# Last tile's logits ahead of the late tiles' conversions, and gathered blocks and late tiles interleaved, in a three-stage attention, MoE and softplus kernel

## The chip, the cores and the metric

One core of one Trainium2 chip. The metric is the device time of one launch in microseconds. All times inside a trace are counted from the start of the profiled span. The engines are PE (matrix products), ACT, DVE and POOL (elementwise work), and SP, which only issues transfers; POOL and ACT issue some too. Each engine takes its instructions in the order in which they were written and stops at one whose input isn't there.

## What is computed

Three layers follow each other on 2304 tokens (4 batches of 576) with 512 features:

```python
# 1 attention, 8 heads, windowed or dilated mask
scores = np.where(masks[None], scale * q @ k.transpose(0, 1, 3, 2), -1e9)
x = softmax(scores) @ v                    # -> (2304, 512)
# 2 mixture of 8 experts, one expert for each token
e_idx = np.argmax(x @ w_gate, axis=1)
for e in range(8):
    h = np.maximum(x[mask_e] @ w1[e], 0.0)
    out[mask_e] = gate_w[mask_e, None] * eom[mask_e, e, None] * (h @ w2[e])
# 3 dense layer with softplus between two products
g = np.maximum(h, 0.0) + np.log1p(np.exp(-np.abs(h)))      # h = out @ w_in
y = g @ w_out
```

## The kernel before

**Attention by tiles.** The tokens are cut into 20 tiles (tile 14 and tile 19, the fifth of their batches, have 64 rows, the others of interest here 128). A loop runs over steps i = 0 to 21. Step i starts tile i, finishes the attention of tile i-1, and for tile i-2 transposes x on PE (`transpose_x`, L485, into `px`) and copies it on ACT (`evict_x`, L496, into `xT`). Steps 20 and 21 are the tail, in which no new tile starts.

**Routing by groups.** The tiles form six groups; the last, group 5, is tiles 17 to 19. For each group `logits` and `route` take the logits on PE (`pl`, L506, from `xT`), transpose them (`lt` L522 and L525 on DVE, `plt` L528 on PE), pick each token's expert on DVE (L565 to L616), count places with five small matmuls (`prk`, L592 to L596), and end with each token's place and its factor in `pair` (L616). They are written as a generator whose steps are interleaved with other work; `("go", 5, n)` in the table of events takes n steps of it, `pump()` takes a few.

**The first expert's rows.** The expert that is computed first (rank 0) is picked before all tiles are routed. Its tokens, up to 424, are brought into `xacc`, four blocks of 128 features by 424 places (c = 0 to 3), transposed and scaled, in two ways that add up in the same accumulators:

- Tokens of tiles 0 to 13 are gathered from memory by POOL's indirect transfers into `xg` 0 to 3 (three of 128 rows, one of 40), and `mm_gathered` multiplies each with a diagonal matrix (L962), one matmul of the order's listing for each c and block.
- Tokens of the late tiles 14 to 19 are loaded by SP (`load_late`, L982, tile `xl0`), scaled and split in two on ACT and DVE (`split_late`: `h` L993, `l` L995), and multiplied with a 0/1 selection matrix (`sel_late`, `sel`, L1004; `mm_late`, L1014). That is two matmuls of 424 columns for each c and late tile. Tiles 14 and 19 share one pair of buffers, one half each.

`xl0` has five buffers for six late tiles; the load of tile 19 waits for the buffer of tile 15, which is free after `l` of tile 15. When `xacc` is complete, `split_rank0` copies it to `xh` on ACT (L1027) and takes the rest as `xl` on DVE (L732), four pieces each. The first expert's first product (`ph`, L894) starts after the last of them. `wl` (L732 as well) is the low part of the first expert's weights; when one is done SP may load the next weight piece.

**Order.** It is written out by hand: engines run what the Python code emits, in that order. Events are put at places of the loop with `at(step, place, ...)`: `ll` is `load_late`, `se` `sel_late`, `sp` `split_late`, `mg` `mm_gathered`, `az` a first matmul that zeroes `xacc` 0 or 1, `q` a `wl`. After the loop a list `late` emits the rest of the late work.

Of the kernel before, what the change touches and what calls it, by code (L numbers as in the profile page):

```python
# [21 lines left out]
P = 128  # L22
# [15 lines left out]
CAPS = [424, 392, 344, 328, 312, 288, 280, 256]  # L38
# [4 lines left out]
def attn_moe_softplus_kernel(ctx: ExitStack, tc: tile.TileContext, q, k, v, w_gate, w_ogate, w1, w2, w_in, w_out, out, dbg=None):  # L43
    nc = tc.nc
# [9 lines left out]
    NC = DM // P  # L54
# [3 lines left out]
    GROUPS = [(0, 4), (4, 8), (8, 11), (11, 14), (14, 17), (17, 20)]  # L58
# [274 lines left out]
    bg, PUMP = [], [2, 1]  # L333

    def pump(times=None):
        for e in bg[: PUMP[1]]:
            if e[1] > 0:
                e[1] -= 1
                continue
            for _ in range(PUMP[0] if times is None else times):  # L340
                e[1] = next(e[0], None)
                if e[1] is None:
                    bg.remove(e)
                if e[1] != 0:
                    break
# [476 lines left out]
    def piece_lo(r, j, eng=None):  # L822
        d = pieces[r, j]
        sub(eng or nc.vector, d[2], d[0], d[1])
# [4 lines left out]
    xg, xs = {}, {}  # L829

    def ntile(n):
        return (n + P - 1) // P
# [103 lines left out]
    NL = GROUPS[G_DRAM][1]  # L936
    xacc = {}
# [8 lines left out]
    def acc(c):  # L946
        pool, tag = ((ps_s, "s"), (ps_s, "s"), (ps_o, "o"), (ps_t, "tp"))[c]
        xacc[c] = pool.tile([P, 512], F32, tag=tag, name=f"xacc{c}")

    def acc0(c):  # L950
        acc(c)
        zero = bce(cumb[:, 0], CAPS[0] // NE)
        nc.tensor.matmul(xacc[c][:, : CAPS[0]], ones, zero, start=True, stop=False, skip_group_check=True)

    def mm_gathered(cs):
        for c in cs:
            if c not in xacc:
                acc0(c)
        for t in range(ntile(CAPS[0])):
            rows = min(P, CAPS[0] - P * t)  # L960
            for c in cs:
                nc.tensor.matmul(  # L962
                    xacc[c][:, P * t : P * t + rows],
                    xg[0, t][:rows, P * c : P * c + P],
                    xacc["d", t][:rows, :rows],
                    start=False,
                    stop=False,
                    skip_group_check=True,
                )

    def rows_of(i):
        return P if i % NW < NW - 1 else S % P
# [33 lines left out]
    def mm_late(i, cs, which=(0, 1)):  # L1006
        last = i == len(tiles) - 1
        parts, s_ = xacc["l", i], xacc["s", i]
        for c in cs:
            first_ = c not in xacc  # L1010
            if first_:
                acc(c)
            for k_ in which:
                nc.tensor.matmul(  # L1014
                    xacc[c][:, : CAPS[0]],
                    parts[k_][:, P * c : P * c + P],
                    s_,
                    start=first_ and k_ == 0,
                    stop=(last and k_ == 1),
                    skip_group_check=True,  # L1020
                )
# [17 lines left out]
    def load_next():  # L1039

        nload[1] += 1
        while nload[1] and nload[0] < len(order_):
            r, j = order_[nload[0]]
            two = r == NE and j >= DIRECT
            if two and nload[1] < 2:
                break
            if r not in er and r != NE:
                if not K.get("ranked"):
                    break
                er[r] = tab_load(nc.sync, r, NE - 1)  # L1050
            load_piece(r, j, er.get(r))
            nload[0] += 1
            nload[1] -= 1 + two

    def hi_(r, j):
        piece_hi(r, j)

    def lo_(r, j):
        piece_lo(r, j)
        if r != NE or j >= 4:  # L1060
            load_next()
# [18 lines left out]
    n = len(tiles)  # L1080
# [12 lines left out]
    def at(i, s, *evs):  # L1093
        EV.setdefault((i, s), []).extend(evs)

    at(21, 0, ("az", 0), ("az", 1))
    at(21, 1, ("mg", 0))
    for g, (t0, t1) in enumerate(GROUPS):
        if g >= G_FAST:
            for t in range(t0, t1):  # L1100
# [5 lines left out]
    at(18, 4, ("ll", 15))  # L1106
    at(19, 3, ("ll", 16), ("ll", 17))
    at(20, 2, ("sc", 0), ("sc", 1), ("sc", 2), ("sc", 3))
    at(20, 3, ("se", 14), ("se", 15), ("sp", 15, "hl"), ("sp", 14, "h"), ("se", 16), ("sp", 16, "h"), ("ll", 18), ("ll", 19))
    at(21, 1, ("go", 5, 4), ("sp", 16, "l"), ("mg", 1), ("go", 5, 8), ("sp", 14, "l"))  # L1110
    ordering = order()

    def events(i, s):
        for what, *a in EV.get((i, s), ()):
            if what == "r":
                bg.append([group(*a), 0, *a])
            elif what == "pl":
                logits_of(*a)
            elif what == "h":
                hi_(0, *a)  # L1120
            elif what == "q":
                lo_(0, *a)
            elif what == "sc":
                diag_gathered(*a)
            elif what == "az":
                acc0(*a)
            elif what == "mg":
                mm_gathered(a)
            elif what == "ll":
                load_late(*a)  # L1130
            elif what == "go":

                e = next((e for e in bg if e[2] == a[0]), None)
                for _ in range(a[1]):
                    if e in bg:
                        e[1] = next(e[0], None)
                        if e[1] is None:
                            bg.remove(e)
            elif what == "se":
                g = next(g for g, (t0, t1) in enumerate(GROUPS) if t0 <= a[0] < t1)  # L1140
                while any(e[2] == g for e in bg):
                    pump()
                sel_late(*a)
            elif what == "sp":
                split_late(*a)

    for i in range(n + 2):
# [52 lines left out]
        if i == n - 4:  # L1200
            nc.vector.tensor_scalar(K["slots"], K["slots"], e0nt, None, ALU.add)
            K["rt"] = K["rt2"]
    def w_lo(i, j):
        lo_(0, j)

    late = []
    for c in (2, 3):
        late += [(mm_late, 15, (c,), (0,)), (mm_gathered, NL, (c,))]
    late += [(mm_late, 15, (c,), (1,)) for c in (2, 3)] + [(mm_late, 15, (c,)) for c in (0, 1)] + [(mm_late, 16, (c,)) for c in range(NC)]
    late += [(fn, i) for fn in (sel_late, split_late) for i in range(17, n)] + [(w_lo, 17, j) for j in (0, 1)]  # L1210
    late += [(mm_late, 17, (c,)) for c in range(NC)]

    late += [(mm_late, i, (c,)) for i, c in ((n - 2, 0), (n - 2, 1), (n - 1, 0), (n - 1, 1), (n - 2, 2), (n - 1, 2), (n - 2, 3), (n - 1, 3))]
    while late:
        if bg:
            pump()
        fn, i, *a = late[0]
        g = next(g for g, (t0, t1) in enumerate(GROUPS) if t0 <= i < t1)
        if fn is mm_gathered or all(e[2] != g for e in bg):
            late.pop(0)  # L1220
            fn(*a) if fn is mm_gathered else fn(i, *a)
    for fn in deferred:
        fn()
    actx.close()
# [91 lines left out]
    for r in range(NE):  # L1316
        n = CAPS[r]
# [73 lines left out]
    sp = {}  # L1391
# [132 lines left out]
```

## Time and profile before

| what | value |
|---|---|
| median of 3 runs | 814.38 us (814.18 to 817.77) |
| profiled run, its time | 815.12 us |
| its span | 813.5 us (1.62 us lie around it) |
| PE busy | 769.4 us, 95% of the span |
| DVE busy | 566.0 us, 70% |
| ACT busy | 471.8 us, 58% |
| POOL busy | 141.3 us, 17% |
| chain that ended last | PE 61%, DVE 11%, issue 9%, ACT 4%, DMA 2% |

Busy shares are averages over all stages. The page's 40 slices are 20.3 us each; the granted PE clock is full in nearly all of them and 0.8 and 0.7 of full in the seventh and eighth, between 122 and 163 us. The change lies in that stretch.

### The profile page before, as it was taken

How to read it: one execution, taken by the hardware profiler on the slowest of the kernel's cores; microseconds unless marked ns; L12 is line 12 of the kernel's file. 1: busy time of each engine (PE TensorE's matmuls, PEld its weight loads, DVE VectorE, ACT ScalarE, POOL GpSimd, SP SyncE). 2: the span in 40 equal slices, each digit the busy share in tenths (PEclk: the TensorE clock that was granted, in tenths of full speed). 3: DMA queues.
4: the chain of work that ended last, by engine and by line, in shares of the span. 5: the costliest groups of instructions: out<-in, count | busy, mean ns of one | idle time of the engine just before them, and what ended most of it. 6: DMA issues, size and time to landing. Idle time of an engine off the chain costs nothing.

```text
span 813.5 us, 14993 instructions
## 1 busy us (share of the span) xinstructions
PE 769.4 (95%) x5542; PEld 689.8 (85%) x5543; DVE 566.0 (70%) x1112; ACT 471.8 (58%) x909; POOL 141.3 (17%) x170
## 2 busy tenths in 40 slices
PE   6998885999999999999989999999999999999994
PEld 5666664898999999999978888899999999999993
DVE  6867884653577887656798989867656656666662
ACT  4776542344655665566766676656656655655561
POOL 9814433121102001100012121210000001001001
PEclk8999998799999999999999999999999999999998
DMA  9996666255799998769431322310000001001000
GB/s 227 267 249 172 137 163 154 72 194 168 241 285 294 306 306 281 234 195 345 109 103 62 96 67 71 91 65 1 20 7 33 0 1 39 1 1 39 1 1 39
DMA packets 85887, 104.49 MB, mean 128 GB/s; under 512 B 30428, under 2 KB 61404, under 8 KB 85792
## 3 DMA queue, kind: packets, MB, share of 16 engines
q1 hardware_dynamic: 74496, 84.22, 35.9%
q0 software_dynamic: 5104, 13.40, 5.1%
q10 hardware_dynamic: 6192, 5.56, 2.0%
q8 instruction: 65, 1.06, 0.6%
q14 instruction: 30, 0.25, 0.1%
HBM read 83.98 MB, written 19.32 MB: 127 GB/s over the span
## 4 chain that ended last, share of the span: by engine, by line
PE 61%; DVE 11%; issue 9%; ACT 4%; DMA 2%; POOL 1%; ACTq 0%; POOLq 0%; DVEq 0%; SPq 0%
PE q L1433 5%; PE pg L895 5%; PE pg L896 5%; PE pg L894 5%; PE q L1431 5%; PE q L1432 5%; PE ph L890 3%; PE ph L892 3%; PE ph L891 3%; PE py L890 3%; PE py L891 3%; PE py L892 3%; DVE l L1411 2%; DVE l L1409 1%; PE py L894 1%
## 5 line engine op out<-in xcount | busy, mean ns | idle before, releaser
L895 PE MATMUL pg<-xlm,wh 128*128 128x384 f32 x384 | 129.7, 338 | 0.0
L894 PE MATMUL pg<-xhm,wh 128*128 128x384 f32 x384 | 129.4, 337 | 0.1
L896 PE MATMUL pg<-xhm,wl 128*128 128x384 f32 x384 | 129.3, 337 | 0.0
L1433 PE MATMUL q<-wh,gl 128*128 128x512 f32 x288 | 114.3, 397 | 3.8 <-DVE gl L732 3.8
L1431 PE MATMUL q<-wh,gh 128*128 128x512 f32 x288 | 114.2, 397 | 1.4 <-ACT gh L1417 0.9
L1432 PE MATMUL q<-wl,gh 128*128 128x512 f32 x288 | 113.2, 393 | 0.0
L732 DVE TENSOR_TENSOR wl<-wr,wh 128x1024 fp32r<-128x1024 f32 x72 | 87.6, 1218 | 32.9 <-ACT wh L787 32.9
L1417 ACT CAST gh<-l 128x384 fp32r<-128x384 f32 x96 | 49.2, 512 | 100.9 <-DVE l L1411 100.9
L732 DVE TENSOR_TENSOR gl<-l,gh 128x384 fp32r<-128x384 f32 x96 | 56.6, 590 | 41.2 <-ACT gh L1417 39.6
L787 ACT CAST wh<-wr 128x1024 fp32r<-128x1024 f32 x72 | 75.0, 1047 | 15.2 <-ACT y L917 6.0
L894 PEld LDWEIGHTS pg<-xhm,wh 128*128 128x128 f32 x384 | 72.1, 188 | 4.3 <-ACT l L1401 0.4
L895 PEld LDWEIGHTS pg<-xlm,wh 128*128 128x128 f32 x384 | 72.0, 188 | 3.8
L1433 PEld LDWEIGHTS q<-wh,gl 128*128 128x128 f32 x288 | 54.0, 188 | 22.1 <-DVE gl L732 10.1
L1402 DVE TENSOR_SCALAR w<-u 128x384 f32<-128x384 f32 x96 | 34.7, 361 | 54.5 <-ACT u L1400 53.8
L896 PEld LDWEIGHTS pg<-xhm,wl 128*128 128x128 f32 x384 | 72.1, 188 | 0.0
L1440 POOL DMA_INDIRECT out_dram<-o,perm_sb x18 | 18.6, 1034 | 271.9 <-DVE o L259 137.4
L1431 PEld LDWEIGHTS q<-wh,gh 128*128 128x128 f32 x288 | 54.1, 188 | 11.9 <-ACT gh L1417 4.2
L1411 DVE TENSOR_TENSOR l<-l,u 128x384 f32<-128x384 f32 x96 | 62.2, 648 | 2.8
L1432 PEld LDWEIGHTS q<-wl,gh 128*128 128x128 f32 x288 | 54.1, 188 | 8.2
L1399 ACT ACTIVATE u<-pg 128x384 f32<-128x384 f32 x96 | 46.9, 488 | 22.3 <-PE pg L896 21.9
L890 PE MATMUL ph<-xh,wh 128*128 128x392 f32 (+5 forms) x192 | 58.5, 305 | 0.9 <-ACT y L917 0.9
L890 PE MATMUL py<-hh,wh 128*128 128x312 f32 (+8 forms) x192 | 58.5, 304 | 0.0
(205 smaller groups left out, 1763.6 us busy)
## 6 DMA issues: line engine op xcount, KB each, us to landing
wr<-in_moe_w_dram SPq DMA_DIRECT2D x64, 512.0 KB, 5.3
raw<-in_q_dram SPq DMA_DIRECT2D x8, 576.0 KB, 5.8
raw<-in_k_dram SPq DMA_DIRECT2D x8, 576.0 KB, 7.5
x2r<-yT_dram SPq DMA_DIRECT2D x12, 384.0 KB, 3.6
vP<-in_v_dram SPq DMA_DIRECT2D x16, 272.0 KB, 8.3
praw<-in_moe_w_in_dram SPq DMA_DIRECT2D x8, 512.0 KB, 5.0
praw<-in_moe_w_out_dram SPq DMA_DIRECT2D x8, 512.0 KB, 5.5
wr<-in_moe_w_in_dram SPq DMA_DIRECT2D x8, 512.0 KB, 4.0
```

What stands on the lines that cost most here:

```text
L732: e.tensor_tensor(lo, src, hi.bitcast(F32), ALU.subtract)
L787: (eng or nc.scalar.copy)(d[1], d[0])
L890: nc.tensor.matmul(ps if wide else ps[:, :cut], wh, xh if wide else xh[:, :cut], start=wide, stop=False, skip_group_check=True)
L891: nc.tensor.matmul(ps[:, :cut], wh, xl[:, :cut], start=False, stop=False, skip_group_check=True)
L894: nc.tensor.matmul(ps, wh, xh, start=(first and i == 0), stop=False)
L895: nc.tensor.matmul(ps, wh, xl, start=False, stop=False)
L896: nc.tensor.matmul(ps, wl, xh, start=False, stop=(last and i == k - 1))
L1411: nc.vector.tensor_tensor(l, l, u, ALU.subtract)
L1417: nc.scalar.copy(gT[b, f][0], l)
L1431: nc.tensor.matmul(acc[b, t], gh[:, ts_], wh, start=(f == 0), stop=False)
L1432: nc.tensor.matmul(acc[b, t], gh[:, ts_], wl, start=False, stop=False)
L1433: nc.tensor.matmul(acc[b, t], gl[:, ts_], wh, start=False, stop=(f == NF - 1))
```

## The change

The order of emission in the tail is changed; no instruction is added or taken away (the five engines have as many rows as before). `mm_gathered` now takes one gathered block and a list of c, where it took all four blocks. The list `late` behind the loop is gone, and its work stands in the table of events at step 21, among the steps of group 5's routing. In the events of step 20, the splits of tiles 14 to 16 are gone, so that they come after the last `evict_x` at step 21.

```diff
-    def mm_gathered(cs):
+    def mm_gathered(t, cs):
+        rows = min(P, CAPS[0] - P * t)
         for c in cs:
             if c not in xacc:
                 acc0(c)
-        for t in range(ntile(CAPS[0])):
-            rows = min(P, CAPS[0] - P * t)
-            for c in cs:
-                nc.tensor.matmul(
...
-    at(21, 1, ("mg", 0))
...
-    at(20, 3, ("se", 14), ("se", 15), ("sp", 15, "hl"), ("sp", 14, "h"), ("se", 16), ("sp", 16, "h"), ("ll", 18), ("ll", 19))
-    at(21, 1, ("go", 5, 4), ("sp", 16, "l"), ("mg", 1), ("go", 5, 8), ("sp", 14, "l"))
+    at(20, 3, ("se", 14), ("se", 15), ("se", 16), ("ll", 18), ("ll", 19))
+    lo2, hi2 = (0, 1), (2, 3)
+    at(21, 1, ("sp", 15, "h"), ("mg", 0, lo2), ("sp", 15, "l"), ("mg", 1, lo2), ("go", 5, 3), ("ml", 15, (2,)), ("go", 5, 1))
...
-    late = []
-    for c in (2, 3):
-        late += [(mm_late, 15, (c,), (0,)), (mm_gathered, NL, (c,))]
...
-            late.pop(0)
-            fn(*a) if fn is mm_gathered else fn(i, *a)
```

ACT at the end of the loop, as a piece of the difference (minus is before, plus after). `px33` and `px34` are the transposed x of tiles 18 and 19, `h015` is `h` of late tile 15, `rex5` and `rgs5` belong to group 5's routing.

```order
 L598 ACTIVATE rgs4_2183<-rgs4_2183 128x3
-L993 ACTIVATE h015_2290<-xl0_15_2094,pair_72 128x512
-L993 ACTIVATE h014_2294<-xl0_14_2011,pair_72 64x512
-L993 ACTIVATE h016_2299<-xl0_16_2202,pair_72 128x512
-L496 COPY xT5_2147<-px34_2310 128x512
-L578 ACTIVATE rex5_2341<-rd5_2339 128x24
...
+L496 COPY xT5_2147<-px34_2300 128x512
+L991 ACTIVATE h015_2310<-xl0_15_2094,pair_72 128x512
+L991 ACTIVATE h014_2329<-xl0_14_2011,pair_72 64x512
+L578 ACTIVATE rex5_2339<-rd5_2337 128x24
+L598 ACTIVATE rgs5_2335<-rgs5_2335 128x3
+L991 ACTIVATE h016_2369<-xl0_16_2202,pair_72 128x512
```

The last copy of x moves ahead of three conversions, and the conversion of tile 16 moves behind the two ACT steps of the routing.

PE from the last transpose of x on, before. `xacc0` and `xacc1` are c = 0 and 1, `xg0_2` is the third gathered block, `pl5` and `plt5` are group 5's logits and their transpose.

```order
L485 MATMUL px34_2310<-identf_64,x34_2270 128x128 x4
L962 MATMUL xacc0_2306<-diag0_2245,xg0_0_2078 128x128
L962 MATMUL xacc0_2306<-diag1_2247,xg0_1_2080 128x128
L962 MATMUL xacc0_2306<-diag2_2249,xg0_2_2082 128x128
L962 MATMUL xacc0_2306<-diag3_2251,xg0_3_2084 128x40
L506 MATMUL pl5_2156<-xT5_2147,wg_68 32x128 x4
L528 MATMUL plt5_2327<-identf_64,lt5_2324 128x96
L962 MATMUL xacc1_2308<-diag0_2245,xg0_0_2078 128x128
```

The same place after:

```order
L485 MATMUL px34_2300<-identf_64,x34_2270 128x128 x4
L506 MATMUL pl5_2156<-xT5_2147,wg_68 32x128 x4
L960 MATMUL xacc0_2296<-diag0_2245,xg0_0_2078 128x128
L960 MATMUL xacc1_2298<-diag0_2245,xg0_0_2078 128x128
L960 MATMUL xacc0_2296<-diag1_2247,xg0_1_2080 128x128
L960 MATMUL xacc1_2298<-diag1_2247,xg0_1_2080 128x128
L1012 MATMUL xacc2_2321<-sel15_2288,h015_2310 128x424
L1012 MATMUL xacc2_2321<-sel15_2288,l015_2311 128x424
L528 MATMUL plt5_2324<-identf_64,lt5_2318 128x96
```

The logits now stand in front of all gathered blocks; the third and fourth block stand behind tile 15's eight matmuls, and the fourth behind the routing's `prk` too. Tiles 16, 17, 18 and 19 follow, eight matmuls each, c in turn.

DVE from the end of group 5's routing on, after. `sel14` is written a second time here, for tile 19, and `l014` twice, for tiles 14 and 19.

```order
L616 RECIPROCAL pair_72<-rs5_2336 128x3
L993 SCALAR_TENSOR_TENSOR l016_2370<-xl0_16_2202,pair_72,h016_2369 128x512
L1002 TENSOR_SCALAR sel17_2387<-slots_1817,rm25_2333 128x424
L993 SCALAR_TENSOR_TENSOR l017_2390<-xl0_17_2204,pair_72,h017_2389 128x512
L1002 TENSOR_SCALAR sel18_2405<-slots_1817,rm25_2333 128x424
L993 SCALAR_TENSOR_TENSOR l014_2330<-xl0_14_2011,pair_72,h014_2329 64x512
L732 TENSOR_TENSOR wl0_0_2050<-wr0_0_1763,wh0_0_2049 128x1024
L1002 TENSOR_SCALAR sel14_2286<-slots_1817,rm25_2333 64x424
L993 SCALAR_TENSOR_TENSOR l018_2421<-xl0_18_2292,pair_72,h018_2420 128x512
L993 SCALAR_TENSOR_TENSOR l014_2330<-xl0_19_2294,pair_72,h014_2329 64x512
L732 TENSOR_TENSOR wl0_1_2092<-wr0_1_1765,wh0_1_2091 128x1024
```

Before, `l` of tile 16 stood ahead of the routing's steps and `l` of tile 14 in their middle; the three `sel`, then `l` of tiles 17, 18 and 19, then both `wl` followed the reciprocal.

## Rows read from the trace of the kernel before

**Rows 1.** Stretches: length, busy us (instructions) of each engine, PE clock, DMA.
```profile
124.00:131.00 7.00, 5.25 (x92) 4.00 (x89) 4.65 (x24) 1.39 (x4) 3.40 (x5) 1.00 0.57 135
131.00:134.50 3.50, 1.37 (x8) 0.99 (x8) 2.35 (x10) 1.33 (x2) 2.58 (x3) 1.00 0.98 340
...
144.00:151.50 7.50, 7.50 (x27) 6.68 (x26) 6.39 (x16) 2.13 (x4) 1.44 (x9) 0.50 0.10 31
...
158.60:802.90 644.30, 637.50 (x3636) 588.61 (x3636) 452.77 (x802) 388.13 (x756) 63.11 (x53) 1.00 0.36 116
```

**Rows 2.** PE in order of time: start, us, instruction, count, idle time before and releaser.
```profile
131.02 0.66 PE L485 MATMUL px<-identf,x 128*128 128x128 f32 x4 [0.35 <-DVE x L449]
...
135.29 0.80 PE L962 MATMUL xacc<-diag,xg 128*128 128x128 f32 x2 [1.87 <-DMA xg<-x_dram,idx]
...
138.34 1.91 PE L506 MATMUL pl<-xT,wg 128*32 128x128 f32 x8
...
158.64 0.46 PE L894 MATMUL ph<-xh,wh 128*128 128x424 f32 x1 [1.21 <-DVE xl L732]
```

**Rows 3.** Stretches of L1014 alone (two rows), then of L962 alone.
```profile
149.30:151.40 2.10, 2.10 (x7) 1.98 (x6) 0.50 0.29 83
152.07:156.08 4.01, 4.01 (x22) 3.94 (x21) 1.00 0.50 150
...
141.23:143.28 2.05, 2.05 (x8) 1.74 (x8) 0.50 0.11 40
```

**Rows 4.** ACT in order of time.
```profile
131.88 1.33 ACT L993 ACTIVATE h<-xl,pair 128x512 fp32r<-128x512 f32 x2 [3.11 <-DMA xl<-x_dram]
135.96 0.72 ACT L993 ACTIVATE h<-xl,pair 128x512 fp32r<-128x512 f32 x1 [2.75 <-DMA xl<-x_dram]
136.59 0.56 ACT L496 COPY xT<-px 128x512 f32<-128x512 f32 x1
...
143.88 0.20 ACT L598 ACTIVATE rgs<-rgs 128x3 f32<-128x3 f32 x1 [1.20 <-DVE rgs L597]
...
157.44 0.51 ACT L1027 CAST xh<-xacc 128x424 fp32r<-128x424 f32 x1 [0.26 <-PE pcnt L685]
```

**Rows 5.** DVE in order of time.
```profile
132.63 0.75 DVE L995 SCALAR_TENSOR_TENSOR l<-xl,pair,h 128x512 fp32r<-128x512 f32 x1 [0.35 <-ACT h L993]
...
140.29 0.29 DVE L522 COPY lt<-pl 96x128 f32<-96x128 f32 x1 [6.55 <-PE pl L506]
...
141.48 0.20 DVE L565 COPY lg<-plt 128x48 f32<-128x48 f32 x1
...
144.53 0.17 DVE L616 RECIPROCAL pair<-rs 128x3 f32<-128x3 f32 x1
144.62 1.21 DVE L1004 TENSOR_SCALAR sel<-slots,rm 128x424 fp32r<-128x424 f32 x3
...
148.10 2.36 DVE L732 TENSOR_TENSOR wl<-wr,wh 128x1024 fp32r<-128x1024 f32 x2
...
156.10 1.71 DVE L732 TENSOR_TENSOR xl<-xacc,xh 128x424 fp32r<-128x424 f32 x3 [5.57 <-ACT xh L1027]
```

**Rows 6.** Loads of late tiles 16 and 17, then 18, then 19: issues and landings.
```profile
L982 SPq DMA_DIRECT2D xl<-x_dram x2: 422/426/430, 130.4 to 130.9; - x2
...
DMA to landing us min/median/max: 5.5/6.4/7.3
...
L982 SPq DMA_DIRECT2D xl<-x_dram x1: 338/338/338, 135.5 to 135.5; - x1
...
DMA to landing us min/median/max: 5.1/5.1/5.1
...
L982 SPq DMA_DIRECT2D xl<-x_dram x1: 451/451/451, 139.8 to 139.8; - x1
...
DMA to landing us min/median/max: 2.4/2.4/2.4
```

**Rows 7.** POOL in order of time: the last of group 5's scatters of places.
```profile
153.35 0.90 POOL L631 DMA_INDIRECT idx_dram<-pair,rposi  x1 [0.30 <-issue]
```

More of the change, by code (lines that the diff above doesn't have):

```diff
@@ L958, in mm_gathered @@
                 acc0(c)
-        for t in range(ntile(CAPS[0])):
-            rows = min(P, CAPS[0] - P * t)
-            for c in cs:
-                nc.tensor.matmul(
[L963 to L969, printed above, removed]
+            nc.tensor.matmul(
+                xacc[c][:, P * t : P * t + rows],
+                xg[0, t][:rows, P * c : P * c + P],
+                xacc["d", t][:rows, :rows],
+                start=False,
+                stop=False,
+                skip_group_check=True,
+            )
     def rows_of(i):
@@ L1108, in attn_moe_softplus_kernel @@
     at(20, 2, ("sc", 0), ("sc", 1), ("sc", 2), ("sc", 3))
-    at(20, 3, ("se", 14), ("se", 15), ("sp", 15, "hl"), ("sp", 14, "h"), ("se", 16), ("sp", 16, "h"), ("ll", 18), ("ll", 19))
-    at(21, 1, ("go", 5, 4), ("sp", 16, "l"), ("mg", 1), ("go", 5, 8), ("sp", 14, "l"))
+    at(20, 3, ("se", 14), ("se", 15), ("se", 16), ("ll", 18), ("ll", 19))
+    lo2, hi2 = (0, 1), (2, 3)
+    at(21, 1, ("sp", 15, "h"), ("mg", 0, lo2), ("sp", 15, "l"), ("mg", 1, lo2), ("go", 5, 3), ("ml", 15, (2,)), ("go", 5, 1))
+    at(21, 1, ("ml", 15, (3,)), ("sp", 14, "h"), ("go", 5, 8), ("ml", 15, lo2), ("mg", 2, lo2), ("go", 5, 1), ("sp", 16, "h"))
+    at(21, 1, *(("mg", t, hi2) for t in range(3)), ("go", 5, 9), ("sp", 16, "l"), ("se", 17), ("sp", 17, "h"), ("mg", 3, (0, 1, 2, 3)))
+    at(21, 1, *(("ml", 16, (c,)) for c in range(4)), ("sp", 17, "l"), ("se", 18), *(("ml", 17, (c,)) for c in range(4)))
+    at(21, 1, ("sp", 14, "l"), ("q", 0), ("se", 19), ("sp", 18, "hl"), *(("ml", 18, (c,)) for c in range(4)))
+    at(21, 1, ("sp", 19, "hl"), ("q", 1), *(("ml", 19, (c,)) for c in range(4)))
     ordering = order()
@@ L1127, in events @@
             elif what == "mg":
-                mm_gathered(a)
+                mm_gathered(*a)
+            elif what == "ml":
+                mm_late(*a)
             elif what == "ll":
@@ L1202, in attn_moe_softplus_kernel @@
             K["rt"] = K["rt2"]
-    def w_lo(i, j):
-        lo_(0, j)
-    late = []
-    for c in (2, 3):
-        late += [(mm_late, 15, (c,), (0,)), (mm_gathered, NL, (c,))]
[L1209 to L1219, printed above, removed]
-            late.pop(0)
-            fn(*a) if fn is mm_gathered else fn(i, *a)
     for fn in deferred:
```

## The prediction

> **What bounds the kernel now.** I read the stretches first. From 158.6 us to 802.9 us PE is busy 637.5 of 644.3 us at full clock, so whatever lets that stretch begin earlier shortens the kernel by as much. Just before it lies the tail: from 131.0 to 134.5 PE is busy only 1.37 of 3.50 us, and from 144.0 to 151.5 it is busy all the time but at a granted clock of 0.50, that is 1.2 GHz in place of 2.4 [rows 1]. The time in order shows how it came to that. PE's last transpose of x is over at 131.68; then PE meets the gathered blocks, and the third has it waiting until 135.29. The last logits, which need none of these blocks, start at 138.34 and take 1.91 us at the half clock [rows 2]. They could not start at 131.7 either, since the copy of x stands on ACT behind three conversions, the third of which waits for a load until 135.96; the copy runs at 136.59 [rows 4]. Group 5's routing on DVE begins at 140.29 and ends at 144.70, and only then can tiles 17 to 19 be selected [rows 5]. The load of tile 19 had landed at 142.2 (139.8 + 2.4) [rows 6], so routing, not data, was late, and 40 matmuls of 424 columns came on top at a slow clock. The first expert's product starts at 158.64 [rows 2]. I forecast when it starts after the change.
>
> **Prices.** A late matmul costs 2.10 / 6 = 0.35 us at half clock and 4.01 / 21 = 0.19 us at full (counts of the weight loads, since the matmul count has one that began earlier). Four gathered matmuls (eight records) cost 2.05 us at half clock, 0.51 each; at full clock I take half, 0.26 [rows 3]. A conversion costs ACT 0.7 (1.33 for two) and DVE 0.75; a `sel` 0.40 (1.21 for three), a `wl` 1.18 (2.36 for two) [rows 4, 5].
>
> **Copy and logits first.** The copy can start when the transpose is over: 131.74 to 132.3. Logits then take half of 1.91, 0.95 us: 132.35 to 133.3. `h` of tile 15, which ran at 131.88, now follows the copy and ends at 133.0; `l` of tile 15 ends at 133.8. DVE has the logits' `lt` behind that `l`, so `lt` starts at 133.8, where it started at 140.29: 6.5 us earlier. From `lt` to the routing's end (144.70) there were 4.41 us, 0.67 of them for `l` of tile 14, which has moved away: 3.74 are left, and the routing ends at 137.55 [rows 5]. On PE its transpose stands behind the first two blocks (4 x 0.26 from 133.3) and two matmuls of tile 15, free at 134.7; its `lt` is ready at 134.4, so 0.3 us are at risk. `prk` stands behind six more late matmuls and two of the third block: 135.0 + 6 x 0.19 + 2 x 0.26 = 136.7; the routing wants it at 136.4 (1.4 us after `lg`, between 141.48 and 144.53 in the same steps). I take 137.7 for the end of the routing, 7 us earlier than before; ends are 137.5 and 138.2.
>
> **Conversions behind it.** `h` of tile 16 now stands behind the routing's `rgs` on ACT, which ran 0.6 us before the routing's end: it ends near 137.7, its load having landed at 135.9. `l` of 16 is over at 138.45, `sel` of 17 at 138.85. Tile 17 landed at 130.9 + 7.3 = 138.2 [rows 6], so `h` 17 ends at 138.9, `l` 17 at 139.7. DVE then has `sel` 18, `l` 14, `wl`, `sel` 19, `l` 18 in its queue: 0.40 + 0.70 + 1.18 + 0.40 + 0.75 = 3.4, so `l` 18 is over at 143.1. Its load is there at 135.5 + 5.1 = 140.6, in time. `l` 19 needs the load of 142.2 and `h` 19, over at 142.95: it is over at 143.85, and the second `wl` at 145.05. The first `wl` standing ahead of `l` 18 costs 1.18 us of this chain; nothing hides it.
>
> **PE.** After `prk` (137.0) come six gathered matmuls and the four of the last block: 10 x 0.26, until 139.6. All blocks had come and been used before 138.34 [rows 2], so they cost no wait. Tiles 16 and 17 take 16 x 0.19 = 3.05: until 142.65. PE then waits for `l` 18 until 143.1, and 15 matmuls are left: 143.1 + 2.85 = 146.0. The four copies and differences of `xacc` come next. c = 0 is complete 6 matmuls before the end, 144.9; its cast takes 0.5 [rows 4], and the four differences 0.57 each (1.71 for three) [rows 5]: 145.5 + 2.3 = 147.8. The first product starts at 147.85.
>
> **Sum.** 158.64 - 147.85 = 10.8 us. The profiled run took 815.12 us with its span of 813.5, so it would take 804.3; it stands 0.74 above the median of the runs, and against 814.38 the time is 803.6.
>
> **What it adds.** The load of tile 19 now waits for an `l` of tile 15 that stands behind it in the program. That is over at 133.8, and the load went out at 139.8 behind its stores, so this costs nothing; every microsecond by which `l` 15 passes 139.8 would count, with the next weight piece queued behind on SP. That piece now goes out at 142.0 behind the first `wl`, before 149.3: earlier, at no cost. POOL's scatters follow the second `wl`: the last ended 3.8 us after it (154.25 against 150.46) [rows 5, 7] and now at 148.9. In the built program the first expert's first `hh` waits for their landing. PE has three buffers there, 36 matmuls, and would stand only from 147.85 + 6.9 = 154.7, so `hh` must be able to run by 153.6. Landings here took from 2.4 us, with little traffic, to 7.3, when the DMA share was 0.98 [rows 1, 6]: 151.3 to 156.2, that is 0 to 2.6 us of loss. From 144.0 to 151.5 that share is 0.10, so I take the short end, and 0.
>
> **Bounds.** With no wait at all on PE after 134.7 (38 x 0.19 + 12 x 0.26 + 0.6) it would be done at 145.6 and the product would start at 147.4; if casts and differences hid too, 146.3: 12.3 us, 802.1. Half a microsecond each for routing and gathered blocks puts the other end of the plain forecast at 805.5.
>
> **Rivals.** *The clock still falls.* It fell after the stretch with 1.37 of 3.50 us busy, and not in 124 to 131 with 5.25 of 7.00, gaps and all [rows 1]. After the change PE works some 2.9 of the 3.5 us up to 134.5, so by these rows it stays. If it fell at 134.5 and stayed down through the tail, 38 x 0.35 + 12 x 0.51 + 0.6 = 20.0 us would end at 154.5 and the product would start at 155.7: 811.5. Should it rise in the run of tiles 16 to 19, as it rose before in a run of late matmuls alone, some 23 of them are fast again: 808.6. The Trainium skill, "TensorE: Matmul & The Clock Gate", section "A second HAM failure mode: psum-queue depth-cycling", says that short idles between groups of matmuls make the clock go back and forth between its levels, which speaks against many small groups with a wait each. By that rule the time is this rival's; the stretch from 124 to 131 doesn't agree with it.
>
> *Loads come later.* If the load of tile 19 took 7.3 us rather than 2.4, its `l` would end at 148.55 and the product start at 151.6: 807.4. For: early PE work changes nothing in the traffic that made 7.3. Against: the same loads go out at the same times.
>
> *Slower than before.* The half clock, once fallen, holds on in the first expert's product, where a matmul of 424 columns loses (0.35 - 0.19) / 0.35 = 0.46 of its time. It decides when it lasts longer than 2.9 / 0.46 = 6.3 us behind 155.7, that is beyond 162.0; held until 171 it would be 818.5. Against it: before, a run of such matmuls had the clock at full again at 152 [rows 3].
>
> *It doesn't do what it says.* The emitted order shows every move; the one thing that could undo it is a wait on the copy, which has none but the transpose. Then 814.4.
>
> **Chances.** Forecast 0.78; loads or scatters later 0.08; clock 0.11 (0.07 at 808.6, 0.04 at 811.5); slower 0.02; nothing 0.01. The range 802.1 to 807.0 holds the first and most of the second. A measurement of this kernel can tell about 0.5% (4.1 us) from no change, so faster means under 810.3: 0.78 + 0.08 + 0.07 = 0.93; same 0.05; slower 0.02.
>
> **What would show it.** Right: logits near 132.4, `lt` near 133.8, the reciprocal near 137.6, granted clock 1.00 from 131 to 150, a PE wait under a microsecond for `l` 18 near 143, first product near 147.9, and the stretch behind it as long as before (644.3). Wrong: a stretch at 0.50; `lt` late because of `h` 15; a PE wait at `prk` or at the fourth block; `hh` waiting for scatters; or a later stage that gives the gain back.

## The result, and the profile after

The changed kernel takes 807.59 us (median of 6 runs, 807.17 to 808.9), the kernel before 815.32 (814.18 to 819.61): a ratio of 0.9899, 95% interval 0.9874 to 0.9925, or 7.7 us less. Forecast were 10.8 us less; the time lies 0.6 us above the top of the range. The profiled span went from 813.5 to 806.0 us.

The tail came out as forecast almost step by step. Stretches of the changed kernel (length, busy us and instructions of PE, weight loads, DVE, ACT, POOL, then PE clock, DMA share, GB/s):

```profile
124.00:131.00 7.00, 5.28 (x92) 4.04 (x90) 4.63 (x24) 1.39 (x4) 3.06 (x4) 1.00 0.48 144
131.00:134.50 3.50, 2.53 (x17) 1.91 (x18) 2.85 (x12) 1.81 (x3) 2.85 (x3) 1.00 0.91 267
134.50:144.00 9.50, 9.17 (x62) 8.48 (x63) 8.03 (x27) 3.21 (x6) 1.23 (x2) 1.00 0.49 119
144.00:151.50 7.50, 6.03 (x32) 5.49 (x31) 6.30 (x13) 4.59 (x7) 4.62 (x11) 1.00 0.44 123
158.60:795.40 636.80, 628.93 (x3592) 579.81 (x3590) 447.27 (x790) 383.51 (x750) 63.83 (x53) 1.00 0.36 117
```

Against [rows 1], PE is busy 2.53 of the 3.5 us up to 134.5 in place of 1.37, and the clock stays at 1.00 where it was 0.50. The last column but one of the fourth row matters later: the DMA share from 144.0 to 151.5 is 0.44, and was 0.10.

PE of the changed kernel in order of time (start, us, instruction, count, idle time before and what ended it):

```profile
131.04 0.66 PE L485 MATMUL px<-identf,x 128*128 128x128 f32 x4 [0.35 <-DVE x L449]
132.37 1.06 PE L506 MATMUL pl<-xT,wg 128*32 128x128 f32 x8 [0.68 <-ACT xT L496]
133.36 0.71 PE L960 MATMUL xacc<-diag,xg 128*128 128x128 f32 x4
134.33 0.71 PE L960 MATMUL xacc<-diag,xg 128*128 128x128 f32 x4 [0.25 <-DMA xg<-x_dram,idx]
...
143.49 0.47 PE L1012 MATMUL xacc<-sel,l 128*128 128x424 f32 x1 [0.33 <-DVE l L993]
...
148.29 0.46 PE L894 MATMUL ph<-xh,wh 128*128 128x424 f32 x1 [0.84 <-DVE xl L732]
...
156.67 0.47 PE L894 MATMUL ph<-xh,wh 128*128 128x424 f32 x1 [1.20 <-DVE hl L908]
```

The logits start at 132.37, 6.0 us earlier than in [rows 2]; of the waits for gathered blocks 0.25 us are left; the first product starts at 148.29, 10.35 us earlier than at 158.64. The last row is what was not forecast: 8 us into the first expert PE stands for 1.20 us.

What stood there begins on POOL, with group 5's scatters:

```profile
145.83 0.97 POOL L631 DMA_INDIRECT idx_dram<-pair,rposi  x1 [0.79 <-DVE rposi L628]
147.10 0.96 POOL L631 DMA_INDIRECT idx_dram<-pair,rposi  x1 [0.30 <-issue]
148.37 1.94 POOL L631 DMA_INDIRECT idx_dram<-pair,rposi  x1 [0.30 <-issue]
```

and ends on ACT, where the first `hh` waits 5.29 us for their landing. SP's store of the table of places waits for the same landing and goes out at 155.1:

```profile
155.09 0.65 SPq L1310 DMA_DIRECT2D perm_dram<-idx_dram  x1
```

```profile
155.46 0.94 ACT L907 ACTIVATE hh<-ph 128x424 fp32r<-128x424 f32 x2 [5.29 <-DMA idx_dram<-pair,rposi]
```

The third scatter's issue took 1.94 us, the two ahead of it 0.97 and 0.96. DVE runs two `wl` beside it:

```profile
148.30 2.36 DVE L732 TENSOR_TENSOR wl<-wr,wh 128x1024 fp32r<-128x1024 f32 x2
```

In the kernel before DVE is idle beside the three, and they took 0.90 to 0.97 us.

From the first product to PE's last compute it took 647.1 us (148.29 to 795.36), where it took 644.25 (158.64 to 802.89). Laid beside each other, the two traces show PE's lead of 10.35 us shrink to 8.84 over the first `hh`, to 8.22 at the first transpose of rank 1, the second expert (L855, 0.5 us of wait for its gathered rows), rise to 8.47 and fall to 7.53 between 312 and 318 us.

### The profile page after: what moved, and what is told of

It is laid out like the page before. It is cut to its first block, busy times and chain, and to the rows that moved or that the text cites. A ratio compares the mean times of both kernels' runs of the same rounds, so it can differ in the third digit from the quotient of the medians.

```text
span 806.0 us, 14994 instructions
## 1 busy us (share of the span) xinstructions
PE 763.1 (95%) x5542; PEld 683.8 (85%) x5543; DVE 565.3 (70%) x1112; ACT 471.5 (59%) x909; POOL 143.2 (18%) x170
## 3 DMA queue, kind: packets, MB, share of 16 engines
q8 instruction: 65, 1.06, 0.6%
## 4 chain that ended last, share of the span: by engine, by line
PE 52%; DVE 11%; issue 10%; ACT 5%; DMA 2%; POOL 1%; POOLq 0%; ACTq 0%; DVEq 0%
PE pg L895 5%; PE q L1419 5%; PE pg L896 5%; PE pg L894 5%; PE q L1418 5%; PE q L1417 5%; PE ph L890 3%; PE ph L892 3%; PE ph L891 3%; PE py L890 3%; PE py L891 3%; PE py L892 3%; DVE l L1397 2%; DVE l L1395 2%; DVE u L1390 1%
## 5 line engine op out<-in xcount | busy, mean ns | idle before, releaser
L1426 POOL DMA_INDIRECT out_dram<-o,perm_sb x18 | 18.6, 1034 | 271.9 <-DVE o L259 137.4
```

## The experiments

Two things had to be told apart: whether the scatters are what took the gain back, and what the tail's 10.35 us were made of. All these runs, on four chips, took longer than the first ones: 825 to 827 us for the kernel before. On which chip the first ones ran is not on record, so whether it is the chip that differs is not shown. The added time is in the attention; the last transpose of x ends between 143 and 153 us there, by the profile, and at 131.7 in the first two. So I count from that transpose. The table has, from each profile, when it ends; from there to the start of the routing's last reciprocal; from that to the first product; the tail, which is the sum of these two; and from the first product to PE's last compute. The two `scat` kernels, hh_moved and best2 are the changed kernel with edits, first_only and inter_only its two halves; in those whose names end in `_late` or `_late6`, scat_late apart, POOL is held up.

| kernel | transpose ends | to reciprocal | to first product | tail | rest |
|---|---|---|---|---|---|
| before (first profile) | 131.7 | 12.9 | 14.1 | 27.0 | 644.3 |
| changed (first profile) | 131.7 | 6.4 | 10.2 | 16.6 | 647.1 |
| before_p | 152.1 | 7.2 | 10.1 | 17.3 | 644.0 |
| after5 / after_p (changed) | 149.5 / 149.1 | 7.4 / 7.7 | 10.2 / 10.2 | 17.6 / 17.9 | 646.8 / 647.0 |
| scat_early | 147.6 | 8.5 | 10.2 | 18.6 | 644.2 |
| hh_moved | 147.0 | 7.7 | 10.2 | 17.9 | 644.5 |
| scat_late | 150.0 | 8.4 | 10.1 | 18.5 | 647.8 |
| first_only | 153.4 | 6.3 | 10.1 | 16.4 | 644.0 |
| inter_only | 146.9 | 6.6 | 10.1 | 16.6 | 645.7 |
| before_late (hold 15 us) | 144.8 | 25.5 | 14.3 | 39.8 | 644.3 |
| after_late (15 us) | 143.5 | 20.8 | 10.1 | 30.9 | 646.1 |
| clock_up_late (15 us) | 142.8 | 28.1 | 10.1 | 38.2 | 644.5 |
| before_late6 (hold 5 us) | 144.9 | 15.5 | 14.1 | 29.6 | 644.4 |
| after_late6 (5 us) | 151.2 | 7.6 | 10.2 | 17.8 | 646.2 |
| clock_up_late6 (5 us) | 146.5 | 17.6 | 11.6 | 29.2 | 644.5 |
| first_only_late6 (5 us) | 143.2 | 13.7 | 14.5 | 28.2 | 643.9 |
| best2 | 146.4 | 5.9 | 9.2 | 15.1 | 644.2 |

### The scatters

The changed kernel again:

> The changed kernel again, beside the three kernels below. Theory (scatters): the first product starts at 148.3 us as forecast, but the first `hh` stands until group 5's scatters have landed (155.1) and PE stands 1.2 us there; another 0.6 us goes at rank 1's first transpose, because the same late `hh` holds up the table of ranks on DVE; about 0.8 us goes near 312 to 318. Time 807.6, 7.5 to 7.7 below the kernel before. Rival (chance): the losses behind 148.3 differ from run to run, and this profile shows other ones.

Measured: 824.93 us, ratio to the kernel before 0.9987 (0.9967 to 1.0008). The wait at `hh` and the longer rest are there again (646.8); the gain of 7.7 us is not. The three kernels beside it are read against this one.

Scatters right behind the routing (`sx` runs what was put off to the end of the loop):

```diff
-    ... ("go", 5, 9), ("sp", 16, "l"), ("se", 17), ...
+    ... ("go", 5, 9), ("sx",), ("sp", 16, "l"), ("se", 17), ...
```

> The changed kernel with group 5's scatters issued right behind its routing (near 138.5 us) and not after the last `wl` (145.8). Theory (scatters): they have landed before 149, the first `hh` starts when its product is done (near 151), PE doesn't stand at 155.5, and rank 1's transposes don't wait either: 1.3 + 0.6 = 1.9 us less than the changed kernel, 805.7. Rival 1 (what is lost is lost anyway: something else, such as the weight pieces, is next by under a microsecond): 806.5 to 807.6. Rival 2 (the scatters get in the way of the last loads of x, which land at 139.5 and 142.0): tile 19's conversion starts later than 142.0 and the first product later than 148.3.

Measured: 822.4 us, ratio 0.9959 (0.9936 to 0.9982), 2.5 us below the changed kernel, with intervals that overlap; the profile decides. The rest is 644.2, and PE has no wait behind `hh` or for rank 1's gathered rows.

`hh` in other memory:

```diff
-    for nm, bufs in (("y", 2), ("hh", 8), ("rt", 1), ("xg", XG)):
+    for nm, bufs in (("y", 2), ("xg", XG), ("rt", 1), ("hh", 8)):
```

> The changed kernel with `hh` at another place in memory, which group 5's `pair` and `rposi` don't share; scatters and everything else as they were. Theory (scatters, through the shared memory alone): the first `hh` starts near 151 though the scatters land at 155 as before, PE doesn't stand at 155.5, and the time is that of the kernel with early scatters, 805.7. Rival 1: rank 1's gather needs the scatters themselves and still comes 0.6 us late: 806.3. Rival 2 (the wait isn't the shared memory): `hh` still starts at 155.4, 807.6.

Measured: 821.71 us, ratio 0.9948 (0.9927 to 0.9968), 3.2 us below the changed kernel; the rest is 644.5. The scatters of this run are as late as ever. SP's store of the table, which waits for their landing, goes out at 171.43, and the last scatter was issued at 164.95:

```profile
164.95 1.95 POOL L631 DMA_INDIRECT idx_dram<-pair,rposi  x1 [0.30 <-issue]
```

```profile
171.43 0.65 SPq L1310 DMA_DIRECT2D perm_dram<-idx_dram  x1
```

Yet ACT's first `hh` starts at 167.56, as soon as its product is there:

```profile
167.56 0.53 ACT L907 ACTIVATE hh<-ph 128x424 fp32r<-128x424 f32 x1 [0.79 <-issue]
```

So nothing in `hh` needs the scatters' result. It waited because of where its buffer lies. Of the two tiles that the scatters read, only `rposi` can have lain there: its pool is closed before that of `hh` opens, while `pair` is in a pool that stays open to the end. Rank 1's gather came in time too: rival 1 falls.

Scatters behind the four `xl`:

```diff
-    for fn in deferred:
-        fn()
...
     split_rank0()
+    for fn in deferred:
+        fn()
```

> The changed kernel with group 5's scatters issued behind the four `xl`, some 2.8 us later. Theory (scatters): `hh` and the next product start 2.8 us later (158.2 and 159.4), nothing hides it: 810.4. Rival (landing is set by the weight pieces under way, not by the issue): the landing stays near 155 to 156 and the time within 0.8 us of 807.6.

Measured: 827.41 us, ratio 1.0005 (0.9979 to 1.0031), so 2.5 us above the changed kernel, with intervals that overlap. In the trace PE's wait for `hl` (the rest of the product, which DVE takes behind `hh` and which frees the buffer that PE writes next) is 1.0 us longer, not 2.8. PE's waits from 162 to 200 us, in after5 and here (us in total, times, longest):

```profile
PE ph L894 <- DVE hl L908: 1.3, 1, 1.3
```

```profile
PE ph L894 <- DVE hl L908: 2.3, 1, 2.3
```

The first `hh` started 4.6 us after the last scatter's issue (172.1 to 176.75), and 7.2 us in after5 (167.2 to 174.44). A later issue does cost, but the landing isn't a fixed time behind it: each theory had a part. One difference is in sight: here the first of the three scatters stands beside DVE's two `wl`, not the last:

```profile
168.75 1.79 POOL L631 DMA_INDIRECT idx_dram<-pair,rposi  x1 [3.55 <-DMA wr<-in_moe_w_dram]
...
172.11 0.90 POOL L631 DMA_INDIRECT idx_dram<-pair,rposi  x1 [0.30 <-issue]
```

In after5, after_p, hh_moved, inter_only and best2 it is the last, as in the first profile, and its issue took 1.93 to 1.95 us. Whether the `wl` are what makes an issue long, and a landing late, no run tests. The Trainium skill, "DMA: Bandwidth & Descriptors", section "Anatomy of one DMA — SWDGE (gpsimd) path", puts the fixed cost of such a transfer at about 2.0 us. Of the six scatters with a landing on record in the first profile none landed that soon (4.7 us at least, the row is below), so the measurement decides.

### What the tail was made of

Both kernels and the two halves of the change, on one chip:

> The kernel before, profiled beside the changed one. On the chip of the last four runs both kernels took some 10 to 17 us longer, all of it in the attention of the first 150 us. Theory: what the change does is counted from the end of the last transpose of x to the first expert's first product; that stretch was 27.0 us in the kernel before and is so again, whatever the attention in front of it took. Rival: where the attention is slower, the loads and gathered blocks are there earlier relative to that transpose, PE waits less, the clock stays up, and the stretch is 19 to 23 us; then there is less to gain.

> The changed kernel beside it. Theory: the stretch from the last transpose to the first product is 16.6 us again, and what follows it is 2.6 us longer than in the kernel before (scatters). Where the attention in front takes as long in both, the time is 10.4 - 2.6 = 7.8 us below the kernel before; by the rival above it is 0 to 4 us below.

Measured: the kernel before 825.89 us, 0.9992 (0.9962 to 1.0021) against its other runs; the changed one 825.25, 0.9975 (0.995 to 1.0). The rival of the first text holds: the tail of the kernel before is 17.3 us here, not 27.0. PE of before_p:

```profile
150.98 1.11 PE L485 MATMUL px<-identf,x 128*128 128x128 f32 x4
151.89 1.22 PE L962 MATMUL xacc<-diag,xg 128*128 128x128 f32 x8
154.01 1.06 PE L506 MATMUL pl<-xT,wg 128*32 128x128 f32 x8 [0.90 <-ACT xT L496]
```

All four blocks are taken in 1.22 us without a wait, where in [rows 2] the third had PE waiting until 135.29. POOL had issued the gathers from 138.0 on, 14 us ahead of the transpose's end. With 27.0 - 17.3 = 9.7 us of the tail gone, hardly anything is left for the change to take.

The first half alone, in the kernel before; `("mg", 0)` stood ahead of the logits and now stands behind them:

```diff
-    at(21, 1, ("mg", 0))
...
-    at(20, 3, ("se", 14), ("se", 15), ("sp", 15, "hl"), ("sp", 14, "h"), ("se", 16), ("sp", 16, "h"), ("ll", 18), ("ll", 19))
-    at(21, 1, ("go", 5, 4), ("sp", 16, "l"), ("mg", 1), ("go", 5, 8), ("sp", 14, "l"))
+    at(20, 3, ("se", 14), ("se", 15), ("se", 16), ("ll", 18), ("ll", 19))
+    at(21, 1, ("sp", 15, "hl"), ("sp", 14, "h"), ("sp", 16, "h"), ("mg", 0), ("go", 5, 4), ("sp", 16, "l"), ("mg", 1), ("go", 5, 8), ("sp", 14, "l"))
```

> The kernel before with the first half of the change alone: the last copy of x ahead of the conversions of tiles 14 to 16, and the last logits ahead of the gathered blocks, which stay in one piece. Theory (both halves are needed): logits 0.7 us behind the last transpose, but the logits' transpose stands behind the fourth gathered block, 6 us behind the last transpose of x, so the routing ends 3 us earlier than before instead of 6.4. From the last transpose to the first product 18.5 us if the clock stays up, 24 if it falls as before; before 27.0, changed kernel 16.6. Rival (the logits' place is all of it): 16.6 to 17.5.

The second half alone, in the changed kernel; the first two blocks (c = 0 and 1) stand ahead of the logits, and the three conversions left step 21:

```diff
+    at(21, 1, ("mg", 0, (0, 1)), ("mg", 1, (0, 1)))
...
-    at(20, 3, ("se", 14), ("se", 15), ("se", 16), ...)
+    at(20, 3, ("se", 14), ("se", 15), ("sp", 15, "hl"), ("sp", 14, "h"), ("se", 16), ("sp", 16, "h"), ...)
...
```

> The changed kernel with the first half undone: the conversions of tiles 14 to 16 ahead of the last copy of x again, and the first two gathered blocks ahead of the last logits; blocks and late tiles stay interleaved. Theory: the copy waits for the load of tile 16 again (4.9 us behind the last transpose), the routing ends 4.5 us later than in the changed kernel, and the stretch from the last transpose to the first product is 21 us at full clock, 24.5 if the clock falls in the gap behind the second block. Rival (interleaving is all of it): 16.6 to 17.5.

Measured: 825.51 us (0.9959, 0.9932 to 0.9986) and 823.91 (0.9982, 0.9952 to 1.0012), tails of 16.4 and 16.6. With no block late, the tails of all four orders lie within 1.6 us of each other. That does not tell the halves apart; the blocks have to be late for that.

So POOL was held up by 20 pairs of copies from and into its own index tile, ahead of the gathers (6 pairs in a second set):

```diff
             load_idx(0, er[0, 0] * NT, CAPS[0])
+            idle = K["sel"].tile([1, 256], I32, name="idle", bufs=1)
+            for _ in range(20):
+                nc.gpsimd.tensor_copy(idle, idx[0][0:1, 0, 0:1].to_broadcast([1, 256]))
+                nc.gpsimd.tensor_copy(idx[0][0:1, :, 0], idx[0][0:1, :, 0])
```

> The kernel before, with POOL held up some 9 to 10 us (copies of its own index tile) ahead of the four gathers of rank 0, and nothing else changed. On this chip the attention ends near 150 us, not 131.7, the gathered blocks have all come by then, and the tail (last transpose to first product) was 17.3 us. Theory (data late against the last transpose is what made the tail 27.0 us in the first profile): with the gathers late again, PE waits at the blocks up to 6 us behind the transpose, the clock falls there, and the tail is 25 to 27 us, the time 8 to 10 us over the kernel before. Rival (something else made those 27 us): tail 17 to 19 us, time within 2 us of the kernel before.

> The changed kernel with the same hold on POOL. Theory: logits and routing don't stand behind the blocks, tail 16.6 to 18.5 us as without the hold, so it is 7 to 9 us faster than the kernel before with the same hold, as it was in the first profiles. Rival: late blocks hold up the changed order as much, tail 22 us or more, and the two kernels with the hold are within 3 us of each other.

Measured: 837.92 us (1.0159, 1.0133 to 1.0185) and 832.79 (1.0101, 1.0076 to 1.0126). The copies held POOL 15 us, not 9 to 10 (from 140.7 to the first gather at 155.9 in before_late; the 17 us in a text below are too many). The kernel before pays 13.2 us for it, its tail is 39.8 us; the changed kernel is 5.1 us faster (theory 7 to 9, rival under 3), its tail 30.9 (rival 22 or more). At this lateness the changed order stands behind the blocks too: PE waits 12.18 us at its first block, and the routing's transpose stands behind the second.

```profile
157.45 1.22 PE L964 MATMUL xacc<-diag,xg 128*128 128x128 f32 x4 [12.18 <-DMA xg<-x_dram,idx]
```

With zeros multiplied ahead of the blocks (4, 10 and 10 matmuls; in the second set 12, 6, 10 and 10):

```diff
         for t in range(ntile(CAPS[0])):
...
+            for _ in range((0, 4, 10, 10)[t] if 0 in cs else 0):
+                zero = bce(cumb[:, 0], CAPS[0] // NE)
+                nc.tensor.matmul(xacc[0][:, : CAPS[0]], ones, zero, start=False, stop=False, skip_group_check=True)
```

> The kernel before with the same hold on POOL, and 24 matmuls that add zeros ahead of the second, third and fourth block, so that PE is busy while it waits. Theory (the half clock is a cost of its own, beside the late routing): granted clock 1.00 from the last transpose on, the routing still ends 12 to 13 us behind it, the tail is 19.5 to 21.5 us, 5 to 6 us less than with the hold alone. Rival (the clock is a side effect and DVE's chain sets the end): the tail stays within 2 us of the kernel with the hold alone.

Measured: 837.77 us (1.0156, 1.013 to 1.0182), no less than with the hold alone. The zeros didn't cover a wait of 15 us, the clock fell, and they put off the reciprocal by 2.6 us. But the clock had risen again before the reciprocal (at 162.3 us, the reciprocal at 170.9), and so the two stretches from there to the first product, with the same instructions in the same order, give the price of the half clock. The kernel with the hold alone, then with the zeros:

```profile
170.55:184.66 14.11, 12.90 (x55) 11.67 (x53) 8.03 (x14) 4.70 (x8) 3.59 (x11) 0.74 0.23 75
```

```profile
171.10:181.03 9.93, 8.73 (x48) 8.09 (x47) 8.04 (x14) 4.70 (x8) 3.58 (x11) 1.00 0.32 106
```

That is 4.2 us between a mean clock of 0.74 and one of 1.00. The kernel before shows the same in its first profile (144.70 to 158.64, clock 0.75) and the changed one beside it:

```profile
144.70:158.64 13.94, 12.73 (x55) 11.52 (x53) 8.02 (x14) 4.70 (x8) 3.58 (x11) 0.75 0.24 75
```

```profile
138.26:148.29 10.03, 8.23 (x46) 7.16 (x45) 9.26 (x16) 4.89 (x9) 2.68 (x10) 1.00 0.38 122
```

In the table, every profile with the clock full behind the reciprocal has 10.1 or 10.2 us there, in either order; only best2, which moves more, has less. In that stretch the new order of tiles 16 to 19 gives nothing by itself. Of the 10.35 us, 12.9 - 6.4 = 6.5 are the earlier end of the routing and 14.1 - 10.2 = 3.9 the clock. Some of the 6.5 is clock as well: the logits took 1.91 us at half clock and 1.06 at full.

The hold of 5 us:

> The kernel before with POOL held up by 6 copies ahead of rank 0's gathers, in place of 20 (which held it 17 us, and the blocks came 15 to 20 us behind the last transpose): 5 us. On this chip the blocks should then come some 4 to 9 us behind the last transpose, about as they did in the first profile (1.3 to 6.1). Theory (late blocks, then late routing and a half clock): tail 24 to 28 us, time 830 to 833. Rival (a hold of this size is hidden): tail 17 to 19, time 825 to 826.

> The changed kernel with the same 5 us of hold. Theory: the logits, the routing's first half and tile 15 don't stand behind the blocks; tail 17 to 21 us, and 5 to 8 us below the kernel before with the same hold. Rival: the tails of the two differ by less than 3 us.

Measured: 829.09 us (1.0043, 1.0023 to 1.0064) and 826.63 (1.0004, 0.9981 to 1.0027), 2.5 us apart, less than expected. In the profile of the kernel before PE waits for the blocks and then takes the logits at half clock, as in [rows 2]:

```profile
144.22 0.66 PE L485 MATMUL px<-identf,x 128*128 128x128 f32 x4 [0.35 <-DVE x L449]
150.45 0.79 PE L966 MATMUL xacc<-diag,xg 128*128 128x128 f32 x2 [5.58 <-DMA xg<-x_dram,idx]
152.28 1.96 PE L966 MATMUL xacc<-diag,xg 128*128 128x128 f32 x6 [1.03 <-DMA xg<-x_dram,idx]
154.17 1.91 PE L506 MATMUL pl<-xT,wg 128*32 128x128 f32 x8
```

A tail of 17.3 us has become one of 29.6 through later blocks and an earlier transpose. In the profile of the changed kernel the attention ended at 151.2 and the blocks were not late, so it can't be set against this one; the times alone compare the two, and their intervals overlap.

> The kernel before with the same 5 us of hold, and 38 matmuls that add zeros (7 us of them at full clock) ahead of the four blocks, so that PE is busy where it would wait. Theory (the half clock costs by itself, some 5 us of the tail): granted clock 1.00 through the tail, routing as late as with the hold alone, tail 19 to 22 us, time 826 to 829. Rival (the late routing is all of it): clock 1.00, tail within 1.5 us of that with the hold alone.

Measured: 829.77 us (1.0048, 1.0023 to 1.0073), tail 29.2. This one settles nothing. The clock was at 0.50 from 152.6 to 156.0 and from 162.8 to 166.2, and the zeros cost what they saved: the reciprocal is 2.1 us later, the part behind it 2.5 us shorter.

> The kernel before with the last copy of x and the last logits first, blocks in one piece, and the same 5 us of hold. Theory (both halves of the change are needed when blocks are late): the logits come 0.7 us behind the last transpose, but their transpose stands behind the fourth block, so the routing ends 1 to 3 us earlier than in the kernel before with the hold, and the tail is 22 to 26 us. Rival (the first half is all of it): tail and time as the changed kernel with the hold.

Measured: 826.08 us (0.9999, 0.9975 to 1.0024). The logits come at 143.91, 0.7 us behind the transpose, and their transpose at 153.42 behind the fourth block; the reciprocal is 13.7 us behind the last transpose of x, 1.8 less than with the hold alone, and the clock falls all the same:

```profile
143.91 1.06 PE L506 MATMUL pl<-xT,wg 128*32 128x128 f32 x8 [0.68 <-ACT xT L496]
148.34 0.80 PE L966 MATMUL xacc<-diag,xg 128*128 128x128 f32 x2 [3.37 <-DMA xg<-x_dram,idx]
151.15 0.80 PE L966 MATMUL xacc<-diag,xg 128*128 128x128 f32 x2 [2.00 <-DMA xg<-x_dram,idx]
152.11 1.37 PE L966 MATMUL xacc<-diag,xg 128*128 128x128 f32 x4 [0.17 <-issue]
153.42 0.42 PE L528 MATMUL plt<-identf,lt 96*128 96x96 f32 x1
```

By the profile the first half alone gives little when blocks are late (28.2 of 29.6 us): the logits come early, but their transpose still stands behind the fourth block. By the times it is level with the changed kernel under the same hold, whose rest is 2 us longer by the scatters. That both halves are needed is not shown. The second half alone was not run with late blocks, and no profile has the changed kernel with blocks as late as here, where the second came 7.9 us behind the transpose; in the first profile of the kernel before it was 1.3 us.

### A kernel faster than both

`hh` elsewhere, both `wl` later (`lo_(0, 1)` is the second), tiles 18 and 19 interleaved by c:

```diff
-    at(21, 1, ("sp", 14, "l"), ("q", 0), ("se", 19), ("sp", 18, "hl"), *(("ml", 18, (c,)) for c in range(4)))
-    at(21, 1, ("sp", 19, "hl"), ("q", 1), *(("ml", 19, (c,)) for c in range(4)))
+    at(21, 1, ("sp", 14, "l"), ("se", 19), ("sp", 18, "hl"), ("sp", 19, "hl"), ("q", 0))
+    at(21, 1, *(("ml", i_, (c,)) for i_, c in ((18, 0), (18, 1), (19, 0), (19, 1), (18, 2), (19, 2), (18, 3), (19, 3))))
...
     split_rank0()
+    lo_(0, 1)
...
-    for nm, bufs in (("y", 2), ("hh", 8), ("rt", 1), ("xg", XG)):
+    for nm, bufs in (("y", 2), ("xg", XG), ("rt", 1), ("hh", 8)):
```

> The changed kernel with `hh` at a place that group 5's scatters don't share, the two `wl` behind the conversion of tile 19 and behind the four `xl`, and tiles 18 and 19 interleaved by c, so that c = 0 is complete six matmuls earlier. Theory: 2.6 us less behind the first product (no wait for the scatters) and 1.2 to 1.5 us less in the tail: some 4 us below the changed kernel, 821 on this chip, ratio to the kernel before 0.993 or less. Rival (the weight pieces that now go out later are next): the same tail, but the stretch behind the first product stays 646 to 647 us.

Measured: 820.16 us, ratio to the kernel before 0.994 (0.9917 to 0.9963), where the changed kernel had 0.9987 and 0.9975 in the other sets. hh_moved alone had 0.9948 (0.9927 to 0.9968), so by the times the two further edits are not told from it. The rest is 644.2, as expected. Behind the reciprocal it takes 9.2 us, 1.0 less than the changed kernel (1.2 to 1.5 expected). The tail of 15.1 has another 1.5 to 1.8 us less ahead of the reciprocal, where the edit changes nothing: the clock was at 1.00 there, and in after5 and after_p at 0.50 for part of it.

## Why the prediction was off, point by point

**Logits and routing: right.** Logits forecast near 132.4, measured 132.37; `lt` 133.8 and 133.64. The reciprocal was forecast for 137.6 and started at 138.09; the routing ended at 138.26, where 137.7 was forecast and 138.2 was the later of the ends given. The routing's transpose on PE stood behind two matmuls of tile 15, and these behind the second block, which came 0.25 us late.

**Conversions and PE: right within half a microsecond.** PE's wait for `l` of tile 18, forecast to end at 143.1, ended at 143.49; the first product, forecast for 147.85, came at 148.29.

**Clock: right, in this profile.** It stayed at 1.00 from 124 to 151.5; in after_p it was at 0.50 from 146.9 to 153.8, across the end of the last transpose, with the same program. The Trainium skill's rule that short idles between groups of matmuls make the clock go back and forth ("TensorE: Matmul & The Clock Gate", "A second HAM failure mode: psum-queue depth-cycling") is not borne out by this trace: PE had three short waits (0.68, 0.25 and 0.33 us) between 131.7 and 143.5 and the clock did not move. One reading of the trace before was wrong: of the 40 matmuls that the prediction has "at a slow clock" eleven started at half clock, and the rest ran at full from 151.6 on; nothing in the sum rests on it.

**"What it adds": the step that failed.** The price of the scatters' landing was bounded by 0 and 2.6 us, from landings between 151.3 and 156.2, and taken as 0. It landed at 155.1, inside the bounds but 1.5 us behind the 153.6 by which `hh` had to run, and cost 1.5 us at `hh` and 0.6 at rank 1's transpose, which the forecast had not tied to it. Two rows misled it. The bounds came from loads of x on SP [rows 6]; the kernel before has 20 scatters of its own, six of them with a landing on record, and this row of them (line 631, from issue to landing) was not read:

```profile
DMA to landing us min/median/max: 4.7/6.5/9.0
```

With 4.7 and 9.0 from the last issue, forecast for 148.0, the landing is 152.7 to 157.0, and with the median 154.5: a loss of 0.9, not 0. The last issue itself ended at 150.3, not at 148.9, for its 1.94 us. And the short end was chosen for the DMA share of 0.10 from 144.0 to 151.5 in [rows 1], which was the old kernel's. The same paragraph had the weight pieces go out at 142 and not at 149.3, "at no cost": they moved into that stretch, and its share became 0.44. That this share made the landing late is not shown. The runs with early scatters and with `hh` elsewhere gave 2.3 to 2.6 us of the rest back.

**"The stretch behind it as long as before": wrong by 2.8 us**, of which 2.1 are these two waits. For the 0.94 us between 312 and 318 only a part of the cause is in sight. PE stood there for 0.3 and 0.5 us on nothing that the profile names. Steps of 0.9 and 0.7 us came at the same place of the program in after_p and hh_moved, and none in scat_early. What it is stays open.

**The sum.** 10.8 forecast, 0.4 lost in the tail, 2.8 behind it: 7.6, against 7.53 in the traces and 7.7 in the medians. The range left out what its own bound said: with 2.6 us for the landing on top of its 805.5 it would have reached 808.1, past the 807.59 measured. (That 805.5 itself doesn't follow: half a microsecond each for routing and blocks, on 803.6, gives 804.6.)

**What no step spoke of.** That the 10 us hang on blocks that come later than the last transpose was in the argument. That this differs from run to run was not. The forecast took the arrival of the blocks in one profile for the kernel's own. That the run it was measured by had the same arrivals was luck: in the later runs the change is worth 1 to 2 us by the medians, and its intervals (up to 1.0008 and 1.0) reach no change.

## What to carry to other kernels

A change that brings work forward moves the traffic that this work releases as well, so a landing there is to be priced from the same kind of transfer and with what the stretch will hold then, not with the DMA share of the old trace. Before an early stage is freed, look at what its buffers become: here an instruction that needed nothing of a transfer waited 5.3 us for it, because its output lies where the transfer reads. And where a gain rests on data that comes late, ask how late it would be if the stage ahead took a few per cent longer. An order in which nothing stands behind such data cost nothing here when the data was early, but its gain was then small as well.

## What the runs showed that was not expected

The last transpose of x ended at 131.7 us in the first two profiles and at 143 to 153 in all later ones, with a clock of 1.00 from 22 to 134 us in the first and stretches at 0.50 inside the attention in the others. DVE waits there at L449, 3.41 us for one x in before_p, and for some of these waits the profile names no work of this core as what ended them. Why that attention is slower was not tried. A half clock that outlasts a wait cost 4.2 us in a stretch of 10, with PE busy in it 12.90 of 14.11 us. And `hh` could start 4.6 to 7.2 us after the last scatter's issue began, though that scatter carries only the 64 places of tile 19.
